# A chunked-attention and ReGLU kernel on one core: its first two blocks issued as single steps of each engine, with some clearing work moved

## The chip, the cores and the metric

The kernel runs on one NeuronCore of a Trainium2 chip. Five engines with instruction queues of their own work in parallel and wait for each other through semaphores: TensorE (PE, matrix products into PSUM), VectorE (DVE), ScalarE (ACT), GpSimd (POOL) and SyncE (SP, which only issues DMAs here). POOL issues the loads that convert from f32 to f16, ACT the stores of the output, SP the small copies and the transposing DMAs. The metric is the device time of one execution in microseconds; lower is better.

## The reference

Two stages, one after the other. Attention in chunks: batch 4, 8 heads, 768 positions, head size 64. A chunk of 32 queries sees 8 memory rows, 16 positions to its left, its own 32 and 8 to its right.

```
for each chunk c:
    k_full = concat(mem_k, k[c_start-16 : c_end+8])     # cut at the sequence's ends
    v_full = concat(mem_v, v[c_start-16 : c_end+8])
    a = softmax(q_c @ k_full.T / 8)
    out[chunk] = a @ v_full
```

Then a gated feed-forward (FFN) on the 3072 tokens of width 512, with an inner width of 1536:

```
y = (relu(x @ w_gate) * (x @ w_val)) @ w_out
```

Inputs and output are f32 in HBM. The kernel computes products in f16 with f32 accumulation.

## The kernel before

**Blocks.** The 3072 tokens are cut into eight blocks of 384 (`TB`). A block is half of one batch entry's sequence: four groups of three chunks (`NQ = 4`, `QB = 96` queries) times eight heads, which are handled as four head pairs (`hp` 0 to 3).

**A block's attention**, per head pair: transposed keys and queries; scores on PE (L253, or L278 from block 3 on); exponential on ACT; the sum and the weighted values on PE; logarithm and exponential on ACT for the reciprocal of the sum; a product on DVE into `xT`, which holds the block's tokens transposed for the FFN. Blocks 0 and 1 have a form of their own. Their keys and queries arrive as packed rows and are turned by PE (`turn_pe`, L206, and copied to SBUF by DVE in `turn_copy`); block 0's scores have the mask added by a matmul (`step_s0`); the sums come from a matmul with ones (`wide_d`, L296) followed by `Ln` and `Exp` on ACT (L299, L300); the value windows are gathered by PE (`gather_v`, L486, copied by DVE at L489); the weighted values are `wide_v` (L307, product L309). From block 2 on, `step_v` (L316) takes values and sums in one matmul from `vwins`, whose 128 rows per query group are 8 memory rows and up to 120 positions and whose columns are 64 values and 64 ones. For these blocks the windows are filled by DMA: `load_band` on POOL for the positions (L145), `load_mem_v` on SP for the memory rows, one copy for each of the four query groups out of `memv` (L161). Rows that lie before the sequence's start are cleared with `zero`, and the ones are written by `one_words` (both DVE). There are two windows, for even and odd blocks.

**A block's FFN** is 12 units of inner columns (`ffn_unit`: four matmuls for the gate, four for the value, L352; `Relu` on ACT, L358; product on DVE into `gv`, L359) and three output units (`out_unit`, 36 matmuls in all, L378, a copy on ACT and a store).

**Order.** Everything is issued under a manual schedule: each engine executes its instructions in the order in which the program text issues them. Before the part written out by hand come the first loads, the clearing of tables, fillers for PE (`fill`) and `valid`, which makes the row of ones for the sequence's first group. Then block 0's attention, block 0's FFN with block 1's attention between its units, and from block 1's FFN on a general loop (`run`), in which the attention of block n+1 goes between the units of block n: scores at unit `at[hp]`, values two units later, the product three units later. In block 1 (`run` with n = 2), `at` is 2, 5, 8, 11, block 2's turns come one unit before the scores, and the list `clear` is worked off, one entry after each unit.

After unit 8 of block 0 the program clears rows 0 to 23 of the even window's first group (L586) and writes its ones; after unit 11 it clears rows of `k16s` (L597, L598) and of the odd window (L599). The loads of block 2's window and of `wo` follow, then those of block 3.

**PSUM** has a pool `t` of three double banks for block 0's attention, replaced by `f` (four banks: the gate and value of two FFN units) and `s` (one double bank for scores), beside the two fixed banks `xo` and `xs`.

Of the kernel before, what the change touches and what calls it, by code (L numbers as in the profile page):

```python
# [8 lines left out]
F32 = mybir.dt.float32  # L9
F16 = mybir.dt.float16  # L10
# [7 lines left out]
def kernel(  # L18
# [167 lines left out]
    def turn_pe(n, hp):  # L186
        if n != 1:
            pool, tag = (pools["t"], "t") if n == 0 else (pools["s"], "sc")
            ps = pool.tile([128, 2, 512], F32, tag=tag, name="kq_ps")
            kps, qps = ps[:, 0], xs if (n, hp) == (0, 0) else ps[:, 1, 0:TB]  # L190
        else:
            ps, kps, qps = None, bank("k_ps"), bank("q_ps")[:, 0:TB]
        turns[n, hp] = ps, kps, qps
        rk, rq = (t.rearrange("p h (j d) -> p h j d", j=J) for t in rows_of(n))
        sel = sels[n % 2].rearrange("p i t -> p (i t)")


        ksteps, qsteps = (dst.rearrange("p (j r) -> p j r", j=J) for dst in (kps, qps))
        if n < 2:
            ksteps = kps.rearrange("p (i j t) -> p j i t", i=NQ, j=J)  # L200
        if n == 0:
            qsteps = qps.rearrange("p (r j) -> p j r", j=J)
        for t, steps, w in ((rk, ksteps, sel[0:KR + 2]), (rq, qsteps, ident[:QR, :QR])):
            for j in range(J):
                for hh in range(2):
                    nc.tensor.matmul(steps[D * hh:D * hh + D, j], lhsT=t[:, 2 * hp + hh, j], rhs=w,  # L206
                                     start=True, stop=True)

    def turn_copy(n, hp):
        if n not in kTs:  # L210
            kq = turned.tile([128, HP, 512 + TB], F16, tag="kq", name="kq")
            kTs[n] = kq[:, :, 0:512].rearrange("p a (i m) -> p i a m", i=NQ)
            qTs[n] = kq[:, :, 512:].rearrange("p a (i m) -> p i a m", i=NQ)
            turns[n] = kq
        ps, kps, qps = turns.pop((n, hp))
        if n == 0 and hp == 0:
            dve_copy(turns[n][:, hp, 0:512], kps)
            act_copy(q00, qps)
        elif n == 0:
            dve_copy(turns[n][:, hp], ps.rearrange("p a c -> p (a c)")[:, 0:512 + TB])  # L220
        else:
            for src, dst in ((kps, turns[n][:, hp, 0:512]), (qps, turns[n][:, hp, 512:])):
                if n == 1 and src is kps:
                    dve_copy(dst, src)  # L224
                    continue
                dve_copy(dst.rearrange("p (r j) -> p r j", j=J), src.rearrange("p (j r) -> p r j", j=J))
# [29 lines left out]
    def step_s0(n, hp):  # L256

        sc = pools["t"].tile([128, 2, 512], F32, tag="t", name="sc_ps")
        mq = bass.AP(tensor=maskq.tensor, offset=maskq.offset, ap=[maskq.ap[0], [0, NQ], [1, QB]])
        for hh in range(2):  # L260
            nc.tensor.matmul(sc[:, hh, 0:TB].rearrange("p (i m) -> p i m", m=QB), lhsT=maskk, rhs=mq,  # L261
                             start=True, stop=False)
        score_mms(n, hp, sc, False)
        ex = epool.tile([128, 2, NQ, QB], F16, tag="ex", name="ex")
        nc.scalar.activation(ex.rearrange("p h i m -> p h (i m)"), sc[:, :, 0:TB], ACT.Exp, scale=SCALE)
        exs[n, hp] = ex

    def step_s(n, hp):
        sc = pools["s"].tile([128, 2, 512], F32, tag="sc", name="sc_ps")
        view = sc[:, :, 0:TB].rearrange("p a (c m) -> p a c m", m=QB)  # L270
        if n < 3:
            score_mms(n, hp, sc, True)
            ex = epool.tile([128, 2, NQ, QB], F16, tag="ex", name="ex")
            flat, exs[n, hp] = ex, ex
        else:

            for i in range(NQ):
                nc.tensor.matmul(sc[:, i // 2, 192 * (i % 2):192 * (i % 2) + 192], lhsT=kTs[n][:, i, hp, :],  # L278
                                 rhs=qbds[n % 2][:, i, hp].rearrange("p h m -> p (h m)"), start=True, stop=True)
            ex = epool.tile([128, NQ, 2, QB], F16, tag="ex", name="ex")  # L280
            flat, exs[n, hp] = ex.rearrange("p (a b) h m -> p a (b h) m", b=2), ex.rearrange("p i h m -> p h i m")
        for g in range(3):
            s = slice(32 * g, 32 * g + 32)
            nc.scalar.activation(flat[:, :, :, s], view[:, :, :, s], ACT.Exp, scale=SCALE, bias=(bias1 if n == 1 else bias)[:, g:g + 1])  # L284
# [7 lines left out]
    def wide_d(n, hp):  # L292
# [5 lines left out]
        rinv = rpool.tile([128, TB], F32, tag="rw", bufs=4, name="rw")  # L298
        nc.scalar.activation(rinv, xs, ACT.Ln, scale=1.0 / 64.0)  # L299
        nc.scalar.activation(rinv, rinv, ACT.Exp, scale=-1.0, bias=mln64)  # L300
        rinvs[n, hp] = rinv

    def wide_v(n, hp, xo_=xo):
        ex = exs.pop((n, hp))
        for i in range(NQ):
            for hh in range(2):
                nc.tensor.matmul(xo_[D * hh:D * hh + D, QB * i:QB * i + QB], lhsT=vwins[n][:, i, 2 * hp + hh, 0:D],  # L307
                                 rhs=ex[:, hh, i, :], start=True, stop=True)
        nc.vector.tensor_tensor(out=x_of(n)[:, hp, :], in0=xo_, in1=rinvs.pop((n, hp)), op=ALU.mult)  # L309
# [44 lines left out]

    def ffn_close(n):
        for (g_ps, v_ps), m in units[n]:
            gr = grpool.tile([128, TB], F16, name="gr")
            nc.scalar.activation(gr, g_ps, ACT.Relu)  # L358
            nc.vector.tensor_tensor(out=gvs[n][:, m, :], in0=v_ps, in1=gr, op=ALU.mult)  # L359
# [68 lines left out]
    zero(bias, 0.0)  # L428

# [44 lines left out]
    def valid(n, i):  # L474
# [4 lines left out]
        dve_copy(ones[:, 1 + n], xo[:, 0:D])  # L479

    def gather_v(n, h0, pool, tag):

        ps = pool.tile([128, 2, 512], F32, tag=tag, name="vg_ps").rearrange("p a (i c) -> p (a i) c", i=2)
        for i in range(NQ):
            for j in range(J):
                nc.tensor.matmul(ps[32 * j:32 * j + 32, i].rearrange("p (h d) -> p h d", d=D),  # L486
                                 lhsT=sels[n][0:KR + 2, i, :], rhs=rv[:, h0:h0 + 4, D * j:D * j + D],
                                 start=True, stop=True)
        dve_copy(vwins[n][:, :, h0:h0 + 4, 0:D], ps.rearrange("p i (h d) -> p i h d", d=D))  # L489
# [5 lines left out]
    def turn(n, hp):  # L495
        turn_pe(n, hp)
        turn_copy(n, hp)


    with tc.tile_pool(name="tps", bufs=3, space=bass.MemoryType.PSUM) as pools["t"]:  # L500
        fill(11)
        valid(0, 0)
        cast(0, 0, dve_copy)
        cast(1, 0, act_copy)
        turn(0, 0)
        cast(0, 1, dve_copy)
        cast(1, 1, act_copy)
        step_s0(0, 0)
        turn(0, 1)
        wide_d(0, 0)  # L510
        turn(0, 2)
        step_s0(0, 1)
        turn(0, 3)
        step_s0(0, 2)
        wide_d(0, 1)
        step_s0(0, 3)
        fill(2)
        gather_v(0, 0, pools["t"], "t")
        wide_d(0, 2)
        gather_v(0, 4, pools["t"], "t")  # L520
        fill(3)
        wide_d(0, 3)
    pools["f"] = ctx.enter_context(tc.tile_pool(name="fps", bufs=4, space=bass.MemoryType.PSUM))
    pools["s"] = ctx.enter_context(tc.tile_pool(name="sps", bufs=1, space=bass.MemoryType.PSUM))
    xo2 = pools["s"].tile([128, 2, 512], F32, tag="sc", name="xo2_ps")
    wide_v(0, 0)
    wide_v(0, 1, xo2[:, 0, 0:TB])


    build_sel(1)  # L530
# [3 lines left out]
    select(bias, NEG, NMEM + 55, [[32, 3]], -1, ALU.is_ge)  # L534
    load_rows_mem(pool_dma, rows_of(1)[0][KR:KR + 2], 1, 0, H)
# [4 lines left out]

    ffn_open(0, (0, 1))
    wide_v(0, 2)
    wide_v(0, 3, xo2[:, 1, 0:TB])
    for f in range(NFC):
        chunk(0, f)
    ffn_close(0)
# [9 lines left out]

    dve_copy(perm.rearrange("p (j t) -> p j t", j=J), ident.rearrange("p (t j) -> p j t", j=J))
    dve_copy(bias16, bias)
    ffn_unit(0, 2, spare=True)
    valid(1, NQ - 1)  # L560
    nc.tensor.matmul(xs[:, 0:3], lhsT=perm, rhs=bias16, start=True, stop=True)
    dve_copy(bias1, xs[:, 0:3])
    ffn_unit(0, 3)
    turn(1, 0)
    turn(1, 1)
    step_s(1, 0)
    turn(1, 2)
    step_s(1, 1)
    turn(1, 3)
    wide_d(1, 0)  # L570
    ffn_unit(0, 4)
    step_s(1, 2)
    wide_d(1, 1)
    ffn_unit(0, 5)
    step_s(1, 3)
    wide_d(1, 2)
    ffn_unit(0, 6)
    wide_d(1, 3)
    gather_v(1, 0, pools["s"], "sc")
    ffn_unit(0, 7)  # L580
    wide_v(1, 0)
    wide_v(1, 1, xs)
    gather_v(1, 4, pools["s"], "sc")
    ffn_unit(0, 8)

    zero(vwins[0][0:NMEM + 16, 0, :, 0:D], 0.0)  # L586
    one_words(0, 0, 128, 0, 1, ONE)
    one_words(0, 0, NMEM + 16, 0, 1, 0)
    one_words(0, 0, NMEM, 0, 1, ONE)
    ffn_unit(0, 9)  # L590
    wide_v(1, 2)
    wide_v(1, 3, xs)
    one_words(0, 0, 128, 1, 2, ONE)
    ffn_unit(0, 10)
    one_words(0, 0, 128, 2, NQ, ONE)
    ffn_unit(0, 11)
    zero(words(k16s[0][0:32, 0].rearrange("p h d -> p (h d)")), 0)  # L597
    zero(words(k16s[1][96:128, NQ - 1].rearrange("p h d -> p (h d)")), 0)  # L598
# [12 lines left out]
    clear = [lambda: one_words(1, 0, 128, 0, NQ, ONE),  # L611
# [12 lines left out]
    def run(order, n, at, turn_at):  # L624
        for u, (b, x) in enumerate(order):
# [5 lines left out]
            unit(b, x, [lambda hp=hp: (turn_pe(n, hp), turn_copy(n, hp)) for hp in turning]  # L631
# [53 lines left out]
```

## Time and profile before

| | us |
|---|---|
| median of five runs | 239.69 |
| lowest and highest | 238.72, 241.51 |
| the profiled execution | 239.69 |
| its span, first to last instruction | 238.0 |
| PE busy | 228.7 |
| ACT busy | 141.5 |
| DVE busy | 110.3 |
| POOL busy | 96.4 |

The span is what the trace covers; the execution's own time is 1.69 us longer. A busy PE is not PE at its peak: [...] the next one starts earlier. So matmul costs are best read as the distance from one start to the next: 0.163 us for an FFN matmul of 384 columns, 0.65 us for a half unit of four. The DMA engines are at work for most of the first 100 us (the page's digits are 7 to 9 there), and only then grow idle.

In the trace's order of time, block 0's first turn starts at 5.81 us, its FFN at 18.17, block 1's first turn at 23.91 and block 1's FFN at 43.95. From there to 232 us PE's matmuls follow each other without a gap.

### The profile page before, as it was taken

What the parts mean: (1) busy time and instruction counts of PE and PEld (TensorE: products, weight loads), DVE (VectorE), ACT (ScalarE), POOL (GpSimd) and SP (SyncE); (2) the same over time, 40 slices, a digit from 0 to 9 for tenths busy, and PEclk for the clock granted to TensorE, in tenths of its full rate; (3) what the DMA queues carried; (4) which work ended last, traced back from release to release, by engine and by line L of the source; (5) the groups of instructions that cost most, each with busy time, mean ns of one, the idle gap of its engine ahead of it and who ended that gap; (6) DMA issues with size and microseconds to landing.
All of it is one profiled execution on the core that took longest, in us unless ns stands there. A gap on an engine that the chain in (4) does not pass through costs nothing.

```text
span 238.0 us, 4739 instructions
## 1 busy us (share of the span) xinstructions
PE 228.7 (96%) x1809; PEld 132.9 (56%) x1809; DVE 110.3 (46%) x214; ACT 141.5 (59%) x300; POOL 96.4 (41%) x124
## 2 busy tenths in 40 slices
PE   6989789999999999999999999999999999999993
PEld 2645545655544566546664666556664666456641
DVE  2675829989720054603652146504551266313400
ACT  3673593367761478727984489638882798434321
POOL 8877548926059600991089305960040000000000
PEclk9999999999999999999999999999999999999999
DMA  7999999999979999499909994999902100120012
GB/s 168 188 195 196 196 184 141 137 200 144 136 136 149 198 147 119 29 171 151 174 11 153 153 169 53 90 162 119 154 0 90 45 0 3 44 88 3 1 45 88
DMA packets 101033, 27.53 MB, mean 116 GB/s; under 512 B 83122, under 2 KB 98066, under 8 KB 101010
## 3 DMA queue, kind: packets, MB, share of 16 engines
q0 software_dynamic: 76336, 15.12, 75.8%
q1 hardware_dynamic: 20802, 5.55, 19.8%
q10 hardware_dynamic: 3872, 6.56, 8.4%
q8 instruction: 14, 0.23, 0.4%
q14 instruction: 9, 0.07, 0.1%
HBM read 31.06 MB, written 6.29 MB: 157 GB/s over the span
## 4 chain that ended last, share of the span: by engine, by line
PE 90%; ACT 4%; DVE 3%; DMA 1%; issue 1%; DVEq 0%
PE o_ps L378 25%; PE g_ps L352 25%; PE v_ps L352 25%; PE sc_ps L278 3%; PE kq_ps L206 2%; PE xo_ps L399 2%; PE xo_ps L316 2%; PE xs_ps L316 2%; ACT ex L284 1%; PE sc_ps L253 1%; ACT rw L300 1%; PE sc_ps L261 1%; DMA out_dram<-o_sb 1%; DVE kq L224 1%; DVE gv L359 1%; ACT rw L299 1%
## 5 line engine op out<-in xcount | busy, mean ns | idle before, releaser
L359 DVE TENSOR_TENSOR gv<-v_ps,gr 128x384 f16<-128x384 f32 x95 | 52.6, 555 | 95.8 <-ACT gr L358 83.8
L352 PE MATMUL g_ps<-xT,wg 128*128 128x384 f16 x380 | 78.3, 326 | 0.0
L352 PE MATMUL v_ps<-xT,wv 128*128 128x384 f16 x380 | 78.2, 326 | 0.0
L378 PE MATMUL o_ps<-wo,gv 128*128 128x512 f16 x288 | 63.5, 379 | 0.0
L358 ACT ACTIVATE gr<-g_ps 128x384 f16<-128x384 f32 x95 | 45.9, 485 | 23.8 <-PE g_ps L352 14.3
L352 PEld LDWEIGHTS <-wg 128*128 128x128 f16 x384 | 36.4, 98 | 22.8 <-issue 0.4
L352 PEld LDWEIGHTS <-wv 128*128 128x128 f16 x384 | 36.2, 98 | 21.7
L378 PEld LDWEIGHTS <-gv 128*128 128x128 f16 x288 | 28.1, 98 | 32.9
L240 POOL COPY qbd<-qT 64x1536 f16<-64x1536 f16 x10 | 14.6, 1462 | 60.6 <-DMA qT<-q16n 60.3
L387 ACT COPY o_sb<-o_ps 128x512 f32<-128x512 f32 x23 | 13.5, 585 | 39.1 <-PE o_ps L378 33.0
L284 ACT ACTIVATE ex<-sc_ps,bias 128x256 f16<-128x256 f32 x84 | 33.2, 466 | 3.9 <-PE sc_ps L253 3.2
L145 POOL DMA_DIRECT2D vwin<-in_v_dram x24 | 21.7, 930 | 3.6 <-PE g_ps L352 2.4
L325 ACT ACTIVATE rinv<-ln,mln 64x768 f32<-64x768 f32 x24 | 22.2, 923 | 0.0
L320 ACT ACTIVATE ln<-xo_ps 64x384 f32<-64x384 f32 x24 | 11.7, 487 | 16.3 <-PE xs_ps L316 16.3
L145 POOL DMA_DIRECT2D k<-in_k_dram x20 | 17.9, 908 | 0.2 <-DVE vwin L599 0.2
L171 POOL DMA_DIRECT2D q16n<-in_q_dram x20 | 15.5, 797 | 5.9 <-DMA wo<-in_moe_w_out_dram 5.9
L331 DVE TENSOR_TENSOR xT<-xo_ps,rinv 64x384 f16<-64x384 f32 x24 | 13.1, 547 | 10.0 <-ACT rinv L325 10.0
L331 DVE TENSOR_TENSOR xT<-xs_ps,rinv 64x384 f16<-64x384 f32 x24 | 13.2, 552 | 0.7
L316 PEld LDWEIGHTS <-vwin 128*128 128x128 f16 x192 | 10.6, 98 | 3.0
L320 ACT ACTIVATE ln<-xs_ps 64x384 f32<-64x384 f32 x24 | 11.4, 475 | 0.0
L316 PE MATMUL xo_ps<-ex,vwin 128*128 128x96 f16 x96 | 11.1, 206 | 0.0
L316 PE MATMUL xs_ps<-ex,vwin 128*128 128x96 f16 x96 | 11.1, 206 | 0.0
(87 smaller groups left out, 145.0 us busy)
## 6 DMA issues: line engine op xcount, KB each, us to landing
out_dram<-o_sb ACTq DMA_DIRECT2D x23, 256.0 KB
vwin<-in_v_dram POOLq DMA_DIRECT2D x18, 120.0 KB, 9.0
q16n<-in_q_dram POOLq DMA_DIRECT2D x20, 96.0 KB, 5.0
k<-in_k_dram POOLq DMA_DIRECT2D x15, 120.0 KB, 4.2
wg<-in_moe_w_gate_dram POOLq DMA_DIRECT2D x6, 256.0 KB, 8.4
wv<-in_moe_w_val_dram POOLq DMA_DIRECT2D x6, 256.0 KB, 9.0
wo<-in_moe_w_out_dram POOLq DMA_DIRECT2D x3, 512.0 KB, 10.6
rk<-in_k_dram POOLq DMA_DIRECT2D x5, 224.0 KB, 7.1
```

The lines of the kernel that those rows point to most:

```text
L145: pool_dma(dsts[p][NMEM + m0:NMEM + m1, i, :, 0:D], src)
L171: pool_dma(q16s[n][:, i], src)
L240: nc.gpsimd.tensor_copy(qbds[n % 2][s, :, :, hh, :].rearrange("p i a m -> p (i a) m"), qTs[n][s].rearrange("p i a m -> p (i a) m"))
L284: nc.scalar.activation(flat[:, :, :, s], view[:, :, :, s], ACT.Exp, scale=SCALE, bias=(bias1 if n == 1 else bias)[:, g:g + 1])
L316: nc.tensor.matmul((xo, xs)[hh][:, QB * i:QB * i + QB], lhsT=vw[:, i, 2 * hp + hh, :], rhs=ex[:, hh, i, :], start=True, stop=True)
L320: nc.scalar.activation(ln[:, hh], (xo, xs)[hh][D:128], ACT.Ln, scale=1.0 / 64.0)
L325: nc.scalar.activation(rinv, lns.pop((n, hp)), ACT.Exp, scale=-1.0, bias=mln64[0:D, :])
L331: nc.vector.tensor_tensor(out=x_of(n)[D * hh:D * hh + D, hp, :], in0=(xo, xs)[hh][0:D], in1=rinv[:, hh, :], op=ALU.mult)
L352: nc.tensor.matmul(ps[a], lhsT=(wg, wv)[a][:, f, 128 * m:128 * m + 128], rhs=xTs[n][:, f, :], start=(f == 0), stop=(f == NFC - 1))
L358: nc.scalar.activation(gr, g_ps, ACT.Relu)
L359: nc.vector.tensor_tensor(out=gvs[n][:, m, :], in0=v_ps, in1=gr, op=ALU.mult)
L378: nc.tensor.matmul(o_ps, lhsT=gvs[n][:, m, 128 * t:128 * t + 128], rhs=wo[:, m, :], start=(m == 0), stop=(m == NDC - 1))
```

## The change

The helpers that issued the work of several engines at once are split: `turn_pe` and `turn_copy` into `turn_k`, `turn_q`, `copy_k`, `copy_q` and `copy_kq`; `step_s0` into `score_mask`, `score_mms` and `score_exp0`; `step_s` into `score` and `score_exp`; `wide_d` into `wide_d`, `wide_ln` and `wide_e`; `wide_v` into `wide_v` and `wide_m`; `ffn_close` into `ffn_relu` and `ffn_mult`; `gather_v` loses its copy to `copy_v`. The matmuls and their shapes stay as they were; block 0's queries of head pairs 1 to 3 are still copied with their keys. A table `STEPS` gives each step a short name, and two strings list the steps of blocks 0 and 1 in the order in which they are issued. Each engine takes from a string the steps that are its own.

What else moves: 14 fillers run in place of 11, and those in the middle (2 and 3) are gone. The copies of `valid`'s result and of `perm`, and POOL's tables, come ahead of the first string, the bias of block 1's last group into it, and it uses another PSUM bank (`xo`). The clearing of `k16s` goes to the start. The even window's `zero` comes after the second string, that is after all of block 0, and its ones become the first three entries of `clear`, in block 1's first units.

```diff
-        fill(11)
+    fill(14)
+    valid(0, 0)
+    dve_copy(ones[:, 1], xo[:, 0:D])
+    dve_copy(perm.rearrange("p (j t) -> p j t", j=J), ident.rearrange("p (t j) -> p j t", j=J))
     build_sel(1)
...
+    zero(words(k16s[0][0:32, 0].rearrange("p h d -> p (h d)")), 0)
+    zero(words(k16s[1][96:128, NQ - 1].rearrange("p h d -> p (h d)")), 0)
...
+    STEPS = {
+        "castk": lambda x: cast(0, x, dve_copy), "castq": lambda x: cast(1, x, act_copy),
+        "Tk": lambda x: turn_k(0, x), "Tq": lambda x: turn_q(0, x),
+        "ck0_": lambda x: copy_k(0, 0), "cq0_": lambda x: copy_q(0, 0), "cp": copy_kq,
+        "mk": score_mask, "Sb": lambda x: score_mms(0, x, scs[0, x], False), "eb": score_exp0,
+        "Db": lambda x: wide_d(0, x), "Lb": lambda x: wide_ln(0, x), "Eb": lambda x: wide_e(0, x),
+        "Gb": lambda x: gather_v(0, x, pools["t"], "t"), "cgb": lambda x: copy_v(0, x),
+        "Vb": lambda x: wide_v(0, x, bank_v0(x)), "mb": lambda x: wide_m(0, x), "ch": first_chunk,
+        "b_": lambda x: dve_copy(bias16, bias), "bv_": lambda x: last_bias(),
+        "vc_": lambda x: dve_copy(ones[:, 2], xo[:, 0:D]), "bc_": lambda x: dve_copy(bias1, xo[:, D:D + 3]),
+        "g": lambda x: ffn_half(x, 0), "v": lambda x: ffn_half(x, 1),
+        "r": lambda x: ffn_end(x, ffn_relu), "mu": lambda x: ffn_end(x, ffn_mult),
+        "T": lambda x: (turn_k(1, x), turn_q(1, x)), "ck": lambda x: copy_k(1, x), "cq": lambda x: copy_q(1, x),
+        "S": lambda x: score(1, x), "e": lambda x: score_exp(1, x), "D": lambda x: wide_d(1, x),
+        "L": lambda x: wide_ln(1, x), "E": lambda x: wide_e(1, x),
+        "G": lambda x: gather_v(1, x, pools["s"], "sc"), "cg": lambda x: copy_v(1, x),
+        "V": lambda x: wide_v(1, x, (xo, xs)[x % 2]), "m": lambda x: wide_m(1, x),
...
+        go("""
+        castq0 castk0 castk1 castq1 Tk0 Tq0 Tk1 Tq1 cq0_0 ck0_0 cp1 mk0 mk1 Sb0 Sb1 Tk2 Tq2 eb0 Tk3 Db0 Tq3 cp2
+        eb1 mk2 Sb2 Gb0 Lb0 cp3 b_0 Db1 Gb1 bv_0 cgb0 Eb0 vc_0 eb2 Lb1 Db2 bc_0 mk3 Eb1 Sb3 Lb2 eb3 Vb0 cgb1 mb0 Db3
+        """)
...
+    go("""
+        Vb1 Eb2 Vb3 Vb2 Lb3 Eb3 mb1 ch0 mb2 ch1 mb3 ch2 ch3 g2 r0 mu0 r1 mu1 r2 v2 T0 mu2 cq0 g3 v3 r3 ck0 T1
+        mu3 ck1 S0 T2 e0 cq1 T3 S1 D0 cq2 e1 ck2 g4 v4 r4 S2 cq3 ck3 g6 mu4 L0 D1 e2 g5 v6 r6 L1 S3 mu6 r5 v5 e3
+        D2 g7 L2 r7 E0 mu5 G0 E1 v7 E2 D3 g8 cg0 mu7 L3 G1 v8 r8 V1 mu8 g9 v9 E3 cg1 r9 V0 g11 v11 m1 m0 mu9 V3
+        m3 r11 V2 g10 v10 r10 m2 mu11 mu10
+    """)
 
     zero(vwins[0][0:NMEM + 16, 0, :, 0:D], 0.0)
-    one_words(0, 0, 128, 0, 1, ONE)
-    one_words(0, 0, NMEM + 16, 0, 1, 0)
-    one_words(0, 0, NMEM, 0, 1, ONE)
-    ffn_unit(0, 9)
-    wide_v(1, 2)
-    wide_v(1, 3, xs)
-    one_words(0, 0, 128, 1, 2, ONE)
-    ffn_unit(0, 10)
-    one_words(0, 0, 128, 2, NQ, ONE)
-    ffn_unit(0, 11)
-    zero(words(k16s[0][0:32, 0].rearrange("p h d -> p (h d)")), 0)
-    zero(words(k16s[1][96:128, NQ - 1].rearrange("p h d -> p (h d)")), 0)
     zero(vwins[1][96:128, NQ - 1, :, 0:D], 0.0)
     load_band(2, v, vwins)
     load_mem_v(2)
...
-    clear = [lambda: one_words(1, 0, 128, 0, NQ, ONE),
+    def window0_ones():
+        one_words(0, 0, 128, 0, 1, ONE)
+        one_words(0, 0, NMEM + 16, 0, 1, 0)
+        one_words(0, 0, NMEM, 0, 1, ONE)
+
+    clear = [window0_ones, lambda: one_words(0, 0, 128, 1, 2, ONE), lambda: one_words(0, 0, 128, 2, NQ, ONE),
+             lambda: one_words(1, 0, 128, 0, NQ, ONE),
              lambda: (one_words(1, 96, 128, NQ - 1, NQ, 0), one_words(1, 96, 120, NQ - 1, NQ, ONE))]
```

In the strings `T`, `S`, `e`, `D`, `L`, `E`, `G`, `V` and `m` are block 1's turn, scores, exponential, sums, logarithm, reciprocal, gather, values and product; `g`, `v`, `r` and `mu` are the gate half, the value half, the `Relu` and the product of block 0's FFN units from 2 on, and `ch` are units 0 and 1 together, by slices of the contraction. The order of the loads on POOL stays as it was.

More of the change, by code (lines that the diff above doesn't have):

```diff
@@ L184, in bank, with turn_k @@
         return pools["f"].tile([128, 512], F32, tag="f", name=name)
-    def turn_pe(n, hp):
+    def turn_k(n, hp):
         if n != 1:
@@ L193, in turn_pe, with turn_q, turn_mms, kq_of @@
         turns[n, hp] = ps, kps, qps
[L194 to L209, printed above, removed]
+        steps = kps.rearrange("p (i j t) -> p j i t", i=NQ, j=J) if n < 2 else kps.rearrange("p (j r) -> p j r", j=J)
+        turn_mms(rows_of(n)[0], steps, sels[n % 2].rearrange("p i t -> p (i t)")[0:KR + 2], hp)
+    def turn_q(n, hp):
+        steps = turns[n, hp][2].rearrange("p (r j) -> p j r" if n == 0 else "p (j r) -> p j r", j=J)
+        turn_mms(rows_of(n)[1], steps, ident[:QR, :QR], hp)
+    def turn_mms(t, steps, w, hp):
+        t = t.rearrange("p h (j d) -> p h j d", j=J)
+        for j in range(J):
+            for hh in range(2):
+                nc.tensor.matmul(steps[D * hh:D * hh + D, j], lhsT=t[:, 2 * hp + hh, j], rhs=w,
+                                 start=True, stop=True)
+    def kq_of(n):
         if n not in kTs:
@@ L214, in turn_copy, with copy_k, copy_q, copy_kq @@
             turns[n] = kq
[L215 to L220, printed above, removed]
-        else:
[L222 to L226, printed above, removed]
+        return turns[n]
+    def copy_k(n, hp):
+        src, dst = turns[n, hp][1], kq_of(n)[:, hp, 0:512]
+        if n == 2:
+            src, dst = src.rearrange("p (j r) -> p r j", j=J), dst.rearrange("p (r j) -> p r j", j=J)
+        dve_copy(dst, src)
+    def copy_q(n, hp):
+        src, dst = turns[n, hp][2], kq_of(n)[:, hp, 512:]
+        if (n, hp) == (0, 0):
+            act_copy(q00, src)
+        else:
+            dve_copy(dst.rearrange("p (r j) -> p r j", j=J), src.rearrange("p (j r) -> p r j", j=J))
+    def copy_kq(hp):
+        dve_copy(kq_of(0)[:, hp], turns[0, hp][0].rearrange("p a c -> p (a c)")[:, 0:512 + TB])
+    def turn(n, hp):
+        for step in (turn_k, turn_q, copy_k, copy_q):
+            step(n, hp)
     def turn_dma(n):
@@ L254, in score_mms, with score_mask @@
                                  start=start, stop=start or i == NQ - 1)
-    def step_s0(n, hp):
-        sc = pools["t"].tile([128, 2, 512], F32, tag="t", name="sc_ps")
+    scs = {}
+    def score_mask(hp):
+        sc = scs[0, hp] = pools["t"].tile([128, 2, 512], F32, tag="t", name="sc_ps")
         mq = bass.AP(tensor=maskq.tensor, offset=maskq.offset, ap=[maskq.ap[0], [0, NQ], [1, QB]])
@@ L262, in step_s0, with score_exp0, score @@
                              start=True, stop=False)
[L263 to L270, printed above, removed]
+    def score_exp0(hp):
+        ex = exs[0, hp] = epool.tile([128, 2, NQ, QB], F16, tag="ex", name="ex")
+        nc.scalar.activation(ex.rearrange("p h i m -> p h (i m)"), scs[0, hp][:, :, 0:TB], ACT.Exp, scale=SCALE)
+    def score(n, hp):
+        sc = scs[n, hp] = pools["s"].tile([128, 2, 512], F32, tag="sc", name="sc_ps")
         if n < 3:
             score_mms(n, hp, sc, True)
-            ex = epool.tile([128, 2, NQ, QB], F16, tag="ex", name="ex")
-            flat, exs[n, hp] = ex, ex
         else:
@@ L279, in step_s, with score_exp @@
                                  rhs=qbds[n % 2][:, i, hp].rearrange("p h m -> p (h m)"), start=True, stop=True)
+    def score_exp(n, hp):
+        view = scs[n, hp][:, :, 0:TB].rearrange("p a (c m) -> p a c m", m=QB)
+        if n < 3:
+            flat = exs[n, hp] = epool.tile([128, 2, NQ, QB], F16, tag="ex", name="ex")
+        else:
             ex = epool.tile([128, NQ, 2, QB], F16, tag="ex", name="ex")
@@ L283, in step_s @@
             s = slice(32 * g, 32 * g + 32)
-            nc.scalar.activation(flat[:, :, :, s], view[:, :, :, s], ACT.Exp, scale=SCALE, bias=(bias1 if n == 1 else bias)[:, g:g + 1])
+            nc.scalar.activation(flat[:, :, :, s], view[:, :, :, s], ACT.Exp, scale=SCALE,
+                                 bias=(bias1 if n == 1 else bias)[:, g:g + 1])
+    def step_s(n, hp):
+        score(n, hp)
+        score_exp(n, hp)
     def x_of(n):
@@ L297, in wide_d, with wide_ln, wide_e, wide_v @@
                                  rhs=ex[:, hh, i0:i1, :], start=True, stop=True)
[L298 to L303, printed above, removed]
+    def wide_ln(n, hp):
+        rinvs[n, hp] = rpool.tile([128, TB], F32, tag="rw", bufs=4, name="rw")
+        nc.scalar.activation(rinvs[n, hp], xs, ACT.Ln, scale=1.0 / 64.0)
+    def wide_e(n, hp):
+        nc.scalar.activation(rinvs[n, hp], rinvs[n, hp], ACT.Exp, scale=-1.0, bias=mln64)
+    vbanks = {}
+    def wide_v(n, hp, bank_):
+        vbanks[n, hp] = bank_
         ex = exs.pop((n, hp))
@@ L306, in wide_v, with wide_m @@
             for hh in range(2):
-                nc.tensor.matmul(xo_[D * hh:D * hh + D, QB * i:QB * i + QB], lhsT=vwins[n][:, i, 2 * hp + hh, 0:D],
+                nc.tensor.matmul(bank_[D * hh:D * hh + D, QB * i:QB * i + QB], lhsT=vwins[n][:, i, 2 * hp + hh, 0:D],
                                  rhs=ex[:, hh, i, :], start=True, stop=True)
-        nc.vector.tensor_tensor(out=x_of(n)[:, hp, :], in0=xo_, in1=rinvs.pop((n, hp)), op=ALU.mult)
+    def wide_m(n, hp):
+        nc.vector.tensor_tensor(out=x_of(n)[:, hp, :], in0=vbanks[n, hp], in1=rinvs.pop((n, hp)), op=ALU.mult)
     def step_v(n, hp):
@@ L353, in ffn_mm, with ffn_relu, ffn_mult @@
                          start=(f == 0), stop=(f == NFC - 1))
+    grs = {}
+    def ffn_relu(n, x):
+        (g_ps, v_ps), m = units[n][x]
+        grs[n, m] = grpool.tile([128, TB], F16, name="gr")
+        nc.scalar.activation(grs[n, m], g_ps, ACT.Relu)
+    def ffn_mult(n, x):
+        (g_ps, v_ps), m = units[n][x]
+        nc.vector.tensor_tensor(out=gvs[n][:, m, :], in0=v_ps, in1=grs.pop((n, m)), op=ALU.mult)
     def ffn_close(n):
[L356 to L359, printed above, removed]
+        for x in range(len(units[n])):
+            ffn_relu(n, x)
+            ffn_mult(n, x)
     def ffn_unit(n, m, between=(), spare=False):
@@ L478, in valid, with gather_v @@
                              start=True, stop=True)
-        dve_copy(ones[:, 1 + n], xo[:, 0:D])
-    def gather_v(n, h0, pool, tag):
-        ps = pool.tile([128, 2, 512], F32, tag=tag, name="vg_ps").rearrange("p a (i c) -> p (a i) c", i=2)
+    vgs = {}
+    def gather_v(n, g, pool, tag):
+        ps = vgs[n, g] = pool.tile([128, 2, 512], F32, tag=tag, name="vg_ps").rearrange("p a (i c) -> p (a i) c", i=2)
         for i in range(NQ):
@@ L486, in gather_v, with copy_v @@
                 nc.tensor.matmul(ps[32 * j:32 * j + 32, i].rearrange("p (h d) -> p h d", d=D),
-                                 lhsT=sels[n][0:KR + 2, i, :], rhs=rv[:, h0:h0 + 4, D * j:D * j + D],
+                                 lhsT=sels[n][0:KR + 2, i, :], rhs=rv[:, 4 * g:4 * g + 4, D * j:D * j + D],
                                  start=True, stop=True)
-        dve_copy(vwins[n][:, :, h0:h0 + 4, 0:D], ps.rearrange("p i (h d) -> p i h d", d=D))
+    def copy_v(n, g):
+        dve_copy(vwins[n][:, :, 4 * g:4 * g + 4, 0:D], vgs[n, g].rearrange("p i (h d) -> p i h d", d=D))
     def cast(t, hp, eng):
@@ L493, in cast @@
         eng(dst[0:n, 2 * hp:2 * hp + 2], src[:, 2 * hp:2 * hp + 2])
[L495 to L500, printed above, removed]
-        fill(11)
[L502 to L527, printed above, removed]
+    def last_bias():
+        valid(1, NQ - 1)
+        nc.tensor.matmul(xo[:, D:D + 3], lhsT=perm, rhs=bias16, start=True, stop=True)
+    def ffn_half(m, a):
+        if a == 0:
+            ffn_open(0, (m,), spare=m == 2)
+            opened[m] = units[0]
+        units[0] = opened[m]
+        for f in range(NFC):
+            ffn_mm(0, 0, f, a)
@@ new lines, in ffn_end, with first_chunk, bank_v0 @@
+    def ffn_end(m, step):
+        if m < 2:
+            units[0] = opened[0]
+            step(0, m)
+        else:
+            units[0] = opened[m]
+            step(0, 0)
+    opened = {}
+    def first_chunk(f):
+        if f == 0:
+            ffn_open(0, (0, 1))
+            opened[0] = units[0]
+        chunk(0, f)
+    xo2 = []
+    def bank_v0(hp):
+        return xo2[0][:, hp // 2, 0:TB] if hp % 2 else xo
+    STEPS = {
[15 more added lines that the diff above has]
+        "V": lambda x: wide_v(1, x, (xo, xs)[x % 2]), "m": lambda x: wide_m(1, x),
+        "fill": fill,
+    }
@@ L530, with go @@
+    def go(steps):
+        for step in steps.split():
+            name = step.rstrip("0123456789")
+            STEPS[name](int(step[len(name):]))
+    fill(14)
+    valid(0, 0)
+    dve_copy(ones[:, 1], xo[:, 0:D])
+    dve_copy(perm.rearrange("p (j t) -> p j t", j=J), ident.rearrange("p (t j) -> p j t", j=J))
     build_sel(1)
@@ L534 @@
     select(bias, NEG, NMEM + 55, [[32, 3]], -1, ALU.is_ge)
+    with tc.tile_pool(name="tps", bufs=3, space=bass.MemoryType.PSUM) as pools["t"]:
+        go("""
+        castq0 castk0 castk1 castq1 Tk0 Tq0 Tk1 Tq1 cq0_0 ck0_0 cp1 mk0 mk1 Sb0 Sb1 Tk2 Tq2 eb0 Tk3 Db0 Tq3 cp2
+        eb1 mk2 Sb2 Gb0 Lb0 cp3 b_0 Db1 Gb1 bv_0 cgb0 Eb0 vc_0 eb2 Lb1 Db2 bc_0 mk3 Eb1 Sb3 Lb2 eb3 Vb0 cgb1 mb0 Db3
+        """)
+    pools["f"] = ctx.enter_context(tc.tile_pool(name="fps", bufs=4, space=bass.MemoryType.PSUM))
+    pools["s"] = ctx.enter_context(tc.tile_pool(name="sps", bufs=1, space=bass.MemoryType.PSUM))
+    xo2.append(pools["s"].tile([128, 2, 512], F32, tag="sc", name="xo2_ps"))
     load_rows_mem(pool_dma, rows_of(1)[0][KR:KR + 2], 1, 0, H)
@@ L539 @@
     load_w(768, 1024)
[L541 to L546, printed above, removed]
     load_v_rows(1)
@@ L554 @@
     load_rows(2, 4, 4)
[L557 to L586, printed above, removed]
-    one_words(0, 0, 128, 0, 1, ONE)
-    one_words(0, 0, NMEM + 16, 0, 1, 0)
-    one_words(0, 0, NMEM, 0, 1, ONE)
-    ffn_unit(0, 9)
-    wide_v(1, 2)
-    wide_v(1, 3, xs)
-    one_words(0, 0, 128, 1, 2, ONE)
-    ffn_unit(0, 10)
-    one_words(0, 0, 128, 2, NQ, ONE)
-    ffn_unit(0, 11)
-    zero(words(k16s[0][0:32, 0].rearrange("p h d -> p (h d)")), 0)
-    zero(words(k16s[1][96:128, NQ - 1].rearrange("p h d -> p (h d)")), 0)
+    go("""
[4 more added lines that the diff above has]
+    """)
+    zero(vwins[0][0:NMEM + 16, 0, :, 0:D], 0.0)
     zero(vwins[1][96:128, NQ - 1, :, 0:D], 0.0)
@@ L630, in run @@
             turning = [hp for hp in range(HP) if n == 2 and u == at[hp] - 1]
-            unit(b, x, [lambda hp=hp: (turn_pe(n, hp), turn_copy(n, hp)) for hp in turning]
+            unit(b, x, [lambda hp=hp: turn(n, hp) for hp in turning]
                  + [lambda w=(w, hp): pieces(n, [w]) for hp in now for w in inner])
```

## The prediction

> **What bounds the kernel now.** I read the page's busy rows first, then the table of stretches, then the tensor engine's timeline up to the point where its gaps end, and last the other queues at that point.
>
> ```profile
> PE 228.7 (96%) x1809; PEld 132.9 (56%) x1809; DVE 110.3 (46%) x214; ACT 141.5 (59%) x300; POOL 96.4 (41%) x124
> ...
> PE   6989789999999999999999999999999999999993
> ```
> ```profile
> 10.00:20.00 10.00, 9.04 (x143) 5.01 (x140) 7.07 (x9) 6.15 (x11) 7.80 (x14) 1.00 1.45 195
> 20.00:30.00 10.00, 8.43 (x127) 5.35 (x125) 7.06 (x16) 5.24 (x13) 5.97 (x9) 1.00 1.45 196
> 30.00:40.00 10.00, 8.93 (x110) 5.01 (x105) 5.66 (x9) 7.18 (x18) 5.34 (x8) 1.00 1.50 171
> 40.00:50.00 10.00, 10.00 (x94) 5.87 (x93) 9.13 (x23) 3.92 (x9) 7.86 (x10) 1.00 1.34 151
> ```
>
> The third column is TensorE (PE). From 40 us to the last product it has no gap, so only what makes PE reach block 1's FFN earlier, or opens a gap later, moves the time. The gaps that the new order can close lie before 40 us:
>
> ```profile
> 25.76 0.35 PE L253 MATMUL sc_ps<-kq 64*128 64x96 f16 x8 [0.70 <-DVE kq L226]
> ...
> 27.40 0.35 PE L253 MATMUL sc_ps<-kq 64*128 64x96 f16 x8 [0.77 <-DVE kq L224]
> ...
> 34.41 0.36 PE L296 MATMUL xs_ps<-ex,ones 128*64 128x288 f16 x4 [0.64 <-ACT rw L299]
> ...
> 37.16 0.36 PE L307 MATMUL xo_ps<-ex,vwin 128*64 128x96 f16 x8 [0.44 <-DVE vwin L489]
> ```
>
> PE waits here for a copy or an exponential of the step it has just issued. The fourth view is the one that decides my forecast: VectorE (DVE), SyncE's waits and SyncE's timeline around the loads of block 2's value window.
>
> ```profile
> 40.30 0.27 DVE L586 MEMSET vwin<- 24x256 uint32 x1
> ```
> ```profile
> SPq L161 <- DVE vwin L586: 38.6, 1, 38.6
> ```
> ```profile
> 40.65 4.15 SPq L161 DMA_DIRECT2D vwin<-memv  x4
> ```
> ```profile
> 51.42 0.22 PE L316 MATMUL xo_ps<-ex,vwin 128*128 128x96 f16 x1
> ```
>
> SyncE (SP) stood 38.6 us for the clearing of 24 window rows (L586), then issued the four copies of the memory's value rows (`load_mem_v(2)`, L161). Block 2's first `step_v` (L316, in block 1's unit 4) reads them. In the trace's semaphore records the fourth copy's last update comes at 51.34 us; the pair of matmuls that needs it starts at 51.68. The copies thus take 10.7 us from SP's start to landing, and today they are 0.34 us early.
>
> [...] the 384-column fillers start 0.33 us apart, the same width in the FFN 0.163, and full pace comes only at about 9.0 us[...]. [...] the copies' 128 B packets come at 23 to 38 per half microsecond beside 72 to 99 packets of 1,024 B of `wo`'s load. [...] The trace shows eight late updates for each copy, two of them some 1.5 us behind the rest.
>
> **The change, part by part.** PE costs are start-to-start distances in the timeline.
>
> *Start.* 14 fillers for 11: 3 x 0.33 = 1.0 us at half clock, and `valid` moves from 4.89 to 5.9. The copy of its result and the copy of `perm` now stand ahead of `castk0` on DVE, so that cast goes from 5.33 to about 6.5 and the first turn from 5.81 to 7.0: +1.2 us, though its data (memory and key rows, last updates 4.38 and 4.49) wait. [...] The two zeroings of `k16s` (0.27 each) run before 2.8 us, while DVE idles 2.99 us for `valid`: nothing.
>
> *Block 0's attention.* Walking the new order by hand with durations from the rows (cast 0.4 to 0.7, key copy 0.69, joint copy 1.1, exponential 0.8, logarithm 0.49, reciprocal 0.61, gather copy 1.18, product 0.5; a PE result usable 0.25 after its last issue), DVE sets the pace. With a released clock the starts are `ck0` 7.6, `cp1` 8.65, `cp2` 11.0, `cp3` 12.1, gather copies 13.4 and 14.9, `mb0` 16.05. The first FFN chunk starts near 17.2 with a released clock, 18.0 without (18.17 now), and the fillers dropped (slots 0.43 + 0.59) hide in it.
>
> *Block 0's FFN with block 1's attention.* PE's own sum: 24 halves x 0.65 = 15.6; four times turn 0.42, scores 0.27, sums 0.29, values 0.20 = 4.7; gathers 1.1; bias 0.35 already in the earlier part; some 14 changes of shape x 0.09 = 1.3: 22.7 us. From a chunk at 17.2 that is 39.9; my walk keeps three waits, 0.6 at the last turn (two copies), 0.1 to 0.3 at the next scores and at bank releases, 1.2 in all. Block 1's first unit starts at 41.1, or 41.9 at half clock: I take 41.5 against 43.95, **2.45 us earlier**. Weights permit it: columns 512, 768, 1024 and 1280 have landed at 24.3, 26.8, 31.8 and 35.9, and my walk asks for them at 26.1, 27.9, 34.0 and 38.0. Those loads keep their order on POOL and issue as older ones land (in the trace each waits for the landing of the eighth before it), so a faster PE does not hasten them.
>
> *Window clears moved.* Three groups of ones (about 1.4 us of DVE) come into block 1's first units, 0.8 us of zeroings leave. DVE is at 9.1 of 10 there. The cover is PE's 1.72 us per unit; without it this costs 0.6 at most. I take nothing, because of the next point.
>
> *The clear that SP waits for.* `zero(vwins[0][0:24])` stood after unit 8, 3.65 us before block 1's start. Now it is behind all of block 0, after `mu10`, which ends about 0.75 after block 1's start. So it ends at 41.5 + 0.75 + 0.27 = 42.5, SP starts at 42.6 instead of 40.65, and the four copies, then the memory keys and the next four, queue behind. POOL's loads aren't behind this wait: the band's first load started at 36.49, before the clear. (POOL's fourth key load of block 3 loses its 0.23 us wait for a clear; its data are wanted only by SP's transpose at 58.12.) Landing: 10.7 us again gives 53.3; 1.0 of it was one long issue (1.71 against 0.69), so 52.3; if service by the DMA engines and not the issue set the time, 51.4. I take 52.3. `step_v` would need it at 41.5 + 7.73 = 49.2 (51.68 - 43.95 = 7.73). PE stands about **3.1 us**, with all of unit 4's second half behind it.
>
> *Sum.* -2.45 + 3.1 = +0.65 on the profiled execution's 239.69 us (span 238.0, 1.69 around it), which is also the median of the five runs (238.72 to 241.51): 240.3. An earlier block 1 lengthens the stand by nearly as much, so the result follows the landing rather than the walk: 51.4 gives 239.4, 53.3 gives 241.3.
>
> **Rivals.** (a) The gain stands: the copies land within 6.6 us of SP's start. For: four issues take 2.8 us, and the last output DMA lands in 1.99. Against: the following four copies of the same kind, after the first burst, still needed 5.95 to 6.4 us from the end of issue, under the same `wo` load, which runs to 54.5. Time 239.69 - 2.45 = 237.2. (b) Slower: [...] (c) The order doesn't do what it says: other waits replace those it closes and block 1 starts near 43.9. Then SP starts at 45.0, the copies land at 54.7, PE wants them at 51.6: +3.1, 242.8. Against: every wait in my walk is short.
>
> **How the numbers follow.** Wait takes the gain's place, 239.2 to 241.6: 0.66. (a) 0.13. (b) 0.14, (c) 0.07, both mostly over 242.1. One per cent, 2.4 us, is about what a measurement can tell here. Faster by more 0.12, within 0.67, slower 0.21. Leaving out a tenth on each side: 237.5 to 242.6.
>
> **What would show it.** Right: the first turn later than 5.81; chunks near 17 to 18; the short gaps above gone and block 1's first unit at 41 to 42; then one gap of 2 to 4 us before the first L316-type matmul, ended by a DMA of `vwin<-memv`, SP's first copy at about 42.6, and the two timelines parallel from there. Wrong: no such gap (a); half-pace FFN halves of 1.3 us after it (b); or PE waits spread over block 0 (c).

## The result and the profile after

The changed kernel takes 240.91 us (median of 38 runs, 238.79 to 243.05) against 239.58 (75 runs, 238.58 to 241.51); the ratio is 1.0039, 95% interval 1.0023 to 1.0054. It is slower by 0.4%. Six of its runs, 242.67 to 243.05 us, had a mean granted clock of 0.986 where all others had 0.991 or more; the median has them in it and the ratio leaves them out. The profiled execution took 241.09 us with a span of 239.4.

The page's busy rows of the changed kernel, and its table of stretches (the third column is PE's busy time):

```profile
PE 228.2 (95%) x1807; PEld 131.7 (55%) x1807; DVE 109.9 (46%) x214; ACT 141.6 (59%) x300; POOL 96.4 (40%) x124
...
PE   7889999949999999999999999999999999999993
```
```profile
20.00:30.00 10.00, 9.47 (x130) 5.50 (x130) 6.26 (x12) 6.41 (x16) 5.63 (x8) 1.00 1.45 196
30.00:40.00 10.00, 10.00 (x120) 5.23 (x120) 6.37 (x11) 5.90 (x13) 5.88 (x9) 1.00 1.51 174
40.00:50.00 10.00, 8.46 (x85) 4.93 (x83) 8.42 (x20) 3.54 (x8) 7.97 (x10) 1.00 1.42 154
50.00:60.00 10.00, 8.13 (x76) 4.67 (x76) 5.71 (x12) 6.31 (x14) 5.09 (x6) 1.00 2.04 162
```

From 20 to 40 us PE now has 19.5 busy microseconds of 20, where it had 17.4. But the page's row has a 4 in its ninth slice, and 3.4 us are gone between 40 and 60, where nothing was before. PE's timeline there shows the gaps:

```profile
48.08 0.34 PE L207 MATMUL kq_ps<-ident,rq 96*64 96x96 f16 x8
49.96 0.20 PE L344 MATMUL xo_ps<-ex,vwin 128*128 128x96 f16 x1 [1.54 <-DMA vwin<-memv]
...
50.70 0.20 PE L344 MATMUL xo_ps<-ex,vwin 128*128 128x96 f16 x1 [0.49 <-DMA vwin<-memv]
...
51.41 0.20 PE L344 MATMUL xo_ps<-ex,vwin 128*128 128x96 f16 x1 [0.47 <-DMA vwin<-memv]
...
52.18 0.20 PE L344 MATMUL xo_ps<-ex,vwin 128*128 128x96 f16 x1 [0.52 <-DMA vwin<-memv]
...
60.28 0.34 PE L263 MATMUL sc_ps<-kq 64*128 64x96 f16 x8 [0.66 <-DVE kq L229]
```

Block 2's first `step_v` (L344 now) waits four times, once for each of SP's copies of the memory's value rows. I call these four waits together the stand. DVE's timeline, SP's waits and SP's timeline say why they come then:

```profile
41.70 0.27 DVE L644 MEMSET vwin<- 24x256 uint32 x1
```
```profile
SPq L161 <- DVE vwin L644: 40.0, 1, 40.0
```
```profile
42.06 4.02 SPq L161 DMA_DIRECT2D vwin<-memv  x4
```

The chain that ended last runs, between the turn and the value step, through the fourth of these copies:

```profile
45.39 6.65 DMA vwin<-memv
52.04 0.14 issue
52.18 0.20 PE xo_ps L344
```

Three distances in PE's timeline hold the whole difference. They lie between the start of the span, the first FFN chunk, block 1's first FFN matmul and the first output matmul (L378 or L416). From the last one on the two profiles run alike (173.40 and 173.42 us to the end of the span).

| us | before | after |
|---|---|---|
| start to first FFN chunk | 18.17 | 16.47 |
| chunk to block 1's first FFN matmul | 25.78 | 24.42 |
| block 1's first FFN matmul to first output matmul | 20.63 | 25.08 |
| sum | 64.58 | 65.97 |

The first two lines gain 3.07 us, the third loses 4.45. The sum, 1.39 us, is the difference of the spans (1.40).

### The profile page after: what moved, and what is told of

Read it like the earlier page. It is cut to its first block, busy times and chain, and to the rows that moved or that the text cites. A ratio compares the mean times of both kernels' runs of the same rounds, so it can differ in the third digit from the quotient of the medians.

```text
span 239.4 us, 4735 instructions
## 1 busy us (share of the span) xinstructions
PE 228.2 (95%) x1807; PEld 131.7 (55%) x1807; DVE 109.9 (46%) x214; ACT 141.6 (59%) x300; POOL 96.4 (40%) x124
## 4 chain that ended last, share of the span: by engine, by line
PE 89%; DVE 4%; DMA 4%; ACT 1%; issue 1%; DVEq 0%
PE o_ps L416 25%; PE g_ps L380 25%; PE v_ps L380 25%; DMA vwin<-memv 3%; PE sc_ps L287 3%; PE xo_ps L437 2%; PE xo_ps L344 2%; PE xs_ps L344 2%; PE kq_ps L207 1%; PE sc_ps L263 1%; PE xs_ps L316 1%; PE vg_ps L527 1%; DVE gv L392 1%; DMA out_dram<-o_sb 1%; DVE kq L222 1%
## 5 line engine op out<-in xcount | busy, mean ns | idle before, releaser
L416 PE MATMUL o_ps<-wo,gv 128*128 128x512 f16 x288 | 63.5, 379 | 0.0
L416 PEld LDWEIGHTS <-gv 128*128 128x128 f16 x288 | 28.1, 98 | 32.9
L344 PE MATMUL xo_ps<-ex,vwin 128*128 128x96 f16 x96 | 11.4, 206 | 3.0 <-DMA vwin<-memv 3.0
L344 PEld LDWEIGHTS <-vwin 128*128 128x128 f16 x192 | 10.7, 98 | 6.4 <-issue 2.9
L344 PE MATMUL xs_ps<-ex,vwin 128*128 128x96 f16 x96 | 11.4, 206 | 0.0
```

Of the source, the lines that this page charges most:

```text
L344: nc.tensor.matmul((xo, xs)[hh][:, QB * i:QB * i + QB], lhsT=vw[:, i, 2 * hp + hh, :], rhs=ex[:, hh, i, :], start=True, stop=True)
L416: nc.tensor.matmul(o_ps, lhsT=gvs[n][:, m, 128 * t:128 * t + 128], rhs=wo[:, m, :], start=(m == 0), stop=(m == NDC - 1))
```

## The experiments

Theory W, the prediction's: the clear that SP waits for holds up the copies, and PE stands for them. Its rival, theory D: the window ones that DVE now writes in block 1 take the gain.

**The clear moved up.** In the second string, and nothing else:

```diff
+        "z_": lambda x: zero(vwins[0][0:NMEM + 16, 0, :, 0:D], 0.0),
...
-        Vb1 Eb2 Vb3 Vb2 Lb3 Eb3 mb1 ch0 mb2 ch1 mb3 ch2 ch3 g2 ...
+        Vb1 Eb2 Vb3 Vb2 Lb3 Eb3 mb1 ch0 mb2 ch1 mb3 z_0 ch2 ch3 g2 ...
...
-    zero(vwins[0][0:NMEM + 16, 0, :, 0:D], 0.0)
```

> The changed kernel with one memset moved: the even window's rows 0 to 23 are cleared on DVE right after block 0's last attention product, near 17 us, and not after all of block 0. Theory W (SP's copies of the memory's values are held by that clear, and PE stands for them): SP's first copy starts when memv has landed, near 37 us and not 42.06; the fourth lands near 47, before block 1's unit 4 wants it at 48.1; the stand of 3.6 us is gone and the time is near 237.3 (ratio to before 0.990). Theory D (DVE's extra window ones in block 1 take the gain): the stand at unit 4 stays or moves to another wait, and the time stays within 1 us of 240.9.

Measured: 237.16 us, ratio to before 0.988 (0.9813 to 0.9946). SP's timeline, and all of PE's waits from 40 to 66 us:

```profile
36.43 3.12 SPq L161 DMA_DIRECT2D vwin<-memv  x4
```
```profile
PE sc_ps L263 <- DVE kq L229: 0.7, 1, 0.7
```

The stand is gone, and the median is 3.75 us lower than the changed kernel's. SP's start came as expected; the fourth copy landed at 42.96 (semaphore records) and not near 47, because the copies now run ahead of most of `wo`, whose 1,024-byte packets start at 42.46 in the changed kernel's trace. The 0.7 us gap behind a key copy stays. This profiled execution itself was the slowest of the four runs (239.95): its clock was released only at 13.6 us, so its first chunk starts at 18.88. The stretch from block 1's first FFN matmul to the first output, which the start does not touch, is 21.52 us.

**The same clear moved down in the kernel before.** Behind `ffn_unit(0, 11)` in place of `ffn_unit(0, 8)`.

> The kernel before with the same memset moved down, from behind unit 8 to behind unit 11 of block 0, nothing else. Theory W: SP's first copy goes from 40.65 to about 44.7, the fourth lands near 54.4, and the first value step of block 2 stands from 51.5 for about 2.8 us: time near 242.4 (ratio 1.012). Theory D: nothing else on DVE is later, so the time stays at 239.6 (within 0.3).

Measured: 242.68 us, ratio 1.0088 (1.0052 to 1.0124), where 1.012 was expected. The place of the clear alone makes the old order slower. The profiled execution took 245.23 us; its trace shows half clock for 3.41 us from 11.28 and again from 55.65. Its first FFN chunk starts only at 19.91, and SP's first copy at 46.97, later than the 44.7 expected. In PE's timeline:

```profile
54.17 0.20 PE L316 MATMUL xo_ps<-ex,vwin 128*128 128x96 f16 x1 [0.36 <-DMA vwin<-memv]
...
55.54 0.20 PE L316 MATMUL xo_ps<-ex,vwin 128*128 128x96 f16 x1 [1.13 <-DMA q16n<-in_q_dram]
...
55.63 1.45 PE L352 MATMUL v_ps<-xT,wv 128*128 128x384 f16 x4
56.87 1.49 PE L352 MATMUL g_ps<-xT,wg 128*128 128x384 f16 x4
58.15 1.27 PE L352 MATMUL v_ps<-xT,wv 128*128 128x384 f16 x4
```

The second wait carries the name of a query load, but the matmul doesn't read queries; the semaphore records show the fourth copy of the memory rows landing at 55.41. Behind it two half units start 1.24 and 1.28 us apart and not 0.65. That is what my rival (b) forecast, seen once: half pace behind the stand. That the stand brought it on is not shown. The other drop, at 11.28, also came behind a long wait of PE, 1.31 us for a load of memory keys that ended at 9.81, but the changed kernel's stand, with one wait of 1.54 us, brought no drop in its trace.

**The window ones written again in block 0's tail**, the clear left last:

```diff
-        ... r8 V1 mu8 g9 v9 E3 cg1 r9 V0 g11 v11 m1 m0 mu9 V3
-        m3 r11 V2 g10 v10 r10 m2 mu11 mu10
+        ... r8 V1 mu8 w_0 g9 v9 E3 cg1 r9 V0 g11 v11 m1 m0 mu9 wi_0 V3
+        m3 r11 V2 g10 v10 r10 m2 mu11 wj_0 mu10
...
-    clear = [window0_ones, lambda: one_words(0, 0, 128, 1, 2, ONE), lambda: one_words(0, 0, 128, 2, NQ, ONE),
-             lambda: one_words(1, 0, 128, 0, NQ, ONE),
+    clear = [lambda: one_words(1, 0, 128, 0, NQ, ONE),
```

The steps `w_`, `wi_` and `wj_` write the three groups of ones.

> The changed kernel with the even window's ones written again in block 0's tail (between its last products) and not in block 1's first units; the clear that SP waits for stays last. Theory W: the stand at unit 4 stays at 3.6 us or grows by the 0.3 us that the clear is later; only the second gap of 0.7 us near 60 us, a wait for a key copy on DVE, can go: 240.2 to 241.2. Theory D: most of the loss goes, near 237.5.

Measured: 240.6 us, ratio 1.0021 (0.9986 to 1.0056). PE's waits from 40 to 66 us, all of them:

```profile
PE xo_ps L344 <- DMA vwin<-memv: 2.4, 4, 0.8
```

The stand stays and the key-copy gap is gone: W, with a minor part for D. The last stretch is 23.65 us against 25.08. The time itself does not tell this kernel from the changed one, whose interval of the ratio overlaps; the trace does.

**`wo` loaded later**, behind block 3's keys and queries on POOL:

```diff
             load_q_tokens(n)
+            if n == 3:
+                load_wo()
             load_band(n, v, vwins)
```

`load_wo` holds the three loads, which leave their old place.

> The changed kernel with the three loads of wo behind block 3's key and query loads on POOL instead of ahead of them, so that SP's four copies meet packets of 128 bytes and not of 1,024. If the copies wait their turn beside wo's long packets on the DMA engines, they land within some 6 us of SP's start, near 48.5, the stand falls below 1 us and the time is near 238.2. If the time from start to landing is SP's issue and a fixed latency, they land near 52 as now and the time stays near 240.9. In both cases wo lands near 60, before the output units want it at 66.

Measured: 237.63 us, ratio 0.9867 (0.9826 to 0.9907). SP starts at the same moment, but the fourth copy lands at 48.42. SP's timeline, then PE's:

```profile
42.06 3.13 SPq L161 DMA_DIRECT2D vwin<-memv  x4
```
```profile
48.36 0.22 PE L344 MATMUL xo_ps<-ex,vwin 128*128 128x96 f16 x1
```

No wait is left there. So the long way from issue to landing comes from `wo`'s load beside the copies (10.0 us with it, 6.4 here) and is not a fixed latency, and a second cure exists that never touches the clear. How `wo` lengthens the way is only in part shown: by the trace's packet records, most of the difference passes before the first data packet of the copies starts (last column). Whether it is the size of `wo`'s packets or their amount was not tried apart.

| kernel | SP's first copy | fourth landed | us between | first data packet, us after the start |
|---|---|---|---|---|
| before | 40.65 | 51.34 | 10.7 | 3.70 |
| after | 42.06 | 52.04 | 10.0 | 4.54 |
| ones back | 42.66 | 51.56 | 8.9 | 4.29 |
| before, clear late | 46.97 | 55.41 | 8.4 | 4.17 |
| clear early (ahead of most of `wo`) | 36.43 | 42.96 | 6.5 | 2.26 |
| `wo` later | 42.06 | 48.42 | 6.4 | 1.89 |

**Both repairs together**, the early clear and the ones in block 0's tail:

> The changed kernel with both repairs: the clear that SP waits for near 17 us, and the even window's ones in block 0's tail. If the changed kernel's time is the sum of three terms (3.1 us gained before block 1, 3.6 lost in the stand at unit 4, 0.7 to 0.9 lost to key copies behind the window ones), both losses go and the time is near 236.4 (ratio to before 0.986). If the second gap was a consequence of something else, the time stays at the 237.2 of the early clear alone.

Measured: 236.86 us (four runs, 236.09 to 236.88), ratio 0.9831 (0.979 to 0.9872). The page's rows:

```profile
PE 227.1 (97%) x1807; PEld 131.5 (56%) x1807; DVE 109.6 (47%) x214; ACT 141.4 (60%) x300; POOL 96.4 (41%) x124
...
PE   7889999999999999999999999999999999999993
```

The hole in the ninth slice is closed. The last stretch is 20.63 us, exactly that of the kernel before. This version is faster than both kernels. From the early clear alone (237.16) the times do not tell it apart, since the intervals overlap and 236.86 lies between the two values expected; the traces do. The ones are not free in block 0's tail either: from the first chunk to block 1 it takes 24.67 or 24.68 us with them there, in three traces, and 24.42 without, in three others.

**Eleven fillers in it again** (`fill(14)` to `fill(11)`):

> The previous kernel with 11 fillers in place of 14. If the three fillers only delay the first cast, the first turn comes near 6.0 us and not 7.07 and the time falls by 0.5 to 1.0 us, to about 235.7. If they release the clock earlier, the first turns run at half pace more often and the time is the same or up to 1.5 us longer.

Measured: 237.35 us, ratio 0.986 (0.9813 to 0.9906), an interval that overlaps the last one: undecided, and the fall to 235.7 did not come. The profile suggests why: the clock was released at 4.99 us even with 11 fillers, and the first turn came at 6.24 (6.37 with 14, where it was released at 4.78).

**A control: the kernel before with the clear moved up**, behind `ffn_close(0)`:

> The kernel before with the same memset moved up, behind the products of block 0's first two FFN units. Theory W: the copies land some 4 us earlier, but nothing waited for them there, so the time stays at 239.6 to 239.9 (within 0.4). A rival on the same place: the copies already held PE back in the kernel before, and the time falls by more than 0.5.

Measured: 240.19 us, ratio 0.999 (0.9964 to 1.0017). The copies start at 36.78 and land at 42.58, and the last stretch stays at 20.63 us: in the kernel before they were close to PE's need, but did not hold it. The moved clear has a small price of its own in this trace, a wait of 0.39 us before the bias matmul (26.08 us from chunk to block 1 for 25.78).

**The last longer wait after the first turns**, in the version with both repairs: `r2 v2` to `v2 r2`.

> The kernel with both repairs, and in the second string v2 before r2: unit 2's gate and value share one double bank of PSUM, and in the changed kernel PE stands 0.58 us before v2 for the Relu of the gate half, the only longer wait left after the first turns. If that wait is the order of issue alone, PE passes it and the time falls by 0.6 us, to about 236.2. If the next wait (the turn's bank, or the copies behind it on DVE) takes its place, the time stays at 236.8.

Measured: 236.85 us, ratio 0.9886 (0.9865 to 0.9908), no different from 236.86; its runs of the kernel before were faster too, 239.67. PE's waits from 5 to 66 us:

```profile
PE kq_ps L207 <- DVE rk L536: 0.9, 1, 0.9
PE xs_ps L316 <- ACT ex L278: 0.6, 1, 0.6
PE sc_ps L263 <- DVE kq L232: 0.2, 1, 0.2
```

The 0.58 us wait is gone and part of it comes back at the turn behind it (a start-to-start distance of 0.50 for 0.25). From chunk to block 1 the trace has 24.27 us against 24.67. So about 0.4 us there, too little for these timings to show; the span of this trace is none the less 0.40 us longer (234.79 against 234.38), with 0.79 us more behind the start of the last matmul.

## Why the prediction was right, and where its sizes were off

The forecast, 240.3 with the wait taking the gain's place, stands in mechanism, in place and nearly in size. By its own steps:

*The order.* Predicted 2.45 us earlier at block 1, measured 3.07 (40.89 against 43.95). The walk gave 41.1 with a released clock; the trace has it released at 5.94. The part after the first chunk is the order's own: 24.42 us, and the same in the execution whose clock came at 13.6, against 25.78 before. My walk had it at 23.9. Its waits, 1.2 us in all, came to about 1.1 in PE's distances, though in other places: 0.74 of it lies between unit 2's halves (0.58 of idle). What was short is PE's own sum: in the stream a turn takes 0.52 us where I had 0.42, and three of the four value steps 0.29 where I had 0.20. The part ahead of the first chunk depends on the clock: 16.47 us where I had 17.2, and 18.88 with the late release where I had 18.0. The 1.70 us gained there are thus not shown to be the order's: the kernel before was released at 9.2 in its profile. My two bounds were too close together; I had assumed a release by about 10 us.

*The start.* First turn 7.07 for a predicted 7.0. The two zeroings of `k16s` cost nothing visible.

*The clear that SP waits for.* Predicted SP start 42.6, landing 52.3, stand 3.1; measured 42.06, 52.04 and some 3.55 (25.08 less 20.63 less the 0.89 of the next step). The stand is longer because block 1 began earlier. From start to landing I took 9.7 of a range of 8.8 to 10.7; it was 10.0. That this came so near is partly luck: I had taken the kernel before's one long issue out, and a long issue came again (1.59 us); without one, the kernel with the ones back took 8.9.

*The window ones.* This is the step that failed: I took nothing and bounded it at 0.6. It costs 0.89 us: 21.52 in place of 20.63 for the last stretch, in two kernels without the stand, and 20.63 again when the ones go back. Less the 0.25 us that block 0's tail saves, 0.64 remain. I had looked at block 1's first units only, where the ones stand. But they push the list `clear` back, so that the four 0.70 us clearings of `qbd` meet the key copies of units 7 and 10; the scores behind them start 0.73 and 0.17 us late. DVE's timeline of the changed kernel:

```profile
58.33 0.70 DVE L655 MEMSET qbd<- 64x768 uint32 x1 [0.22 <-issue]
59.06 0.69 DVE L222 CAST kq<-kq_ps 128x512 f16<-128x512 f32 x1
59.67 0.55 DVE L229 CAST kq<-kq_ps 128x384 f16<-128x384 f32 x1
```

The turn's result lay ready at 57.2; the copies end at 60.22, and the scores start at 60.28.

*The sum.* Predicted -2.45 + 3.1 + 0 = +0.65; the profile has -3.07 + 3.55 + 0.89 = +1.37. The medians differ by 1.33 us, the ratio says 0.9. The gain and the stand were each larger than forecast by about half a microsecond, and these two errors nearly cancel; what is left of the difference is the window ones.

*The rivals.* (a) was wrong for the reason given against it: ways of about 6.6 us are reached only where `wo` is not beside the copies (6.4 and 6.5 in the table, 5.8 to 6.8 in the four other kernels with an early clear). (b) did not happen in this profile: the trace's clock record stays at full from 5.94 to 238.04 us, through the stand. What brings the clock down is not shown: in the trace of the late clear it fell to half twice, behind a wait of 1.31 us and behind waits of 0.36 and 1.13 us, while the changed kernel's four waits of 1.54, 0.49, 0.47 and 0.52 us brought no fall. The 0.14 given to (b) was my estimate. Whether (b) happened in other executions stays open. The six runs at a clock of 0.986 took 242.67 to 243.05 us; the profile of the kernel before with the late clear, which has two stretches at half pace, has the same 0.986. But no trace of those six is kept, and none of the 75 runs of the kernel before took more than 241.51. (c) is refuted by the table of distances. My remark that an earlier block 1 only lengthens the stand was not tried by itself; in the table of copies the way beside `wo` is shorter where SP starts later, so the landing need not follow the start one to one.

## What to carry to other kernels

When work is reordered to close gaps, list every instruction that another queue waits for and that changes its place relative to the new order, however small: here a 0.27 us memset put last on DVE released SP, and PE paid 3.6 us for it. A list that is worked off one entry per unit must be checked at its far end, where the pushed entries meet other work. And a gain ahead of a load is only kept if the load's landing has margin: in the kernel before, it was 0.34 us.

## What the runs showed of the hardware that I had not expected

The prediction put the copies' long way down to `wo`'s packets beside theirs. The traces bear this out only in part. The same four copies of 8 KB took 10.0 us from start to landing beside `wo`'s 1,024-byte packets and 6.4 us beside packets of 128 bytes. But 2.65 of these 3.6 us passed before the copies' first data packet started (4.54 us against 1.89). From there to the landing it was 5.4 us against 4.5, and one long issue alone is 0.9 us of that. What holds the first packet back beside `wo` is not shown.

The clock's release scatters more than I had assumed: in the profiles here it came at 4.5, 4.8, 5.4, 5.9, 6.5 and 13.6 us with 14 fillers and at 4.5, 5.0, 9.2 and 9.2 with 11, and the first FFN chunk starts 2.4 us apart in the changed kernel (5.9) and in the one with the clear moved up (13.6). A stand of 3.6 us broken by a pair of matmuls every 0.7 us left the clock at full in the changed kernel's profile (5.94 to 238.04 us).
